# Group 5's q and k: cast on GpSimd and transposed by DMA instead of on TensorE

## The chip, the cores and the metric

The kernel runs on one core of one Trainium2 chip. The metric is the device time of one execution in microseconds, lower is better. The engines in this text: TensorE (PE, with its weight loads as PEld), VectorE (DVE), ScalarE (ACT), GpSimd (POOL) and SyncE (SP), which here does nothing but issue transfers.

## The reference

Chunked attention over 8 batches of 8 heads, 576 positions, head size 64, in chunks of 64, then a feed-forward layer with a squared ReLU:

```python
scores = scale * np.matmul(q_c, k_c.transpose(0, 1, 2, 4, 3))      # per chunk of 64
attn = np.exp(scores - max); attn = attn / (sum(attn) + 1e-09)
x = np.matmul(attn, v_c)  ->  (4608 tokens, 512)
h = np.maximum(x @ w_in, 0.0)                                       # 512 -> 2048
return (h * h) @ w_out                                              # 2048 -> 512
```

## The kernel before

The 4608 tokens are 18 groups of 256; two groups make a block of the feed-forward layer. While block j goes through the feed-forward layer, the attention of block j + 1 is slipped in between its matmuls, and the loads for block j + 2 are issued. A block has 48 slots, one after every four matmuls of TensorE; a plan says what is emitted in which slot. Scores need q and k with the head size on the partitions, so both must be transposed. Groups up to 5 do this on TensorE (`TA`), later ones by DMA (`C`, a cast to bf16 on GpSimd, then `TD`).

```python
FIRST_DMA_T = 6
...
in_pool = ctx.enter_context(tc.tile_pool(name="qk", bufs=5))
att_pool = ctx.enter_context(tc.tile_pool(name="att", bufs=3))
...
def cast_qk(g):                                     # C
    qkb = att_pool.tile([128, 2, 2 * H * D], BF16, name="qkb", bufs=2)
    state["qkb", g] = qkb
    for which in range(2):
        nc.gpsimd.tensor_copy(
            out=qkb[:, which], in_=qk[g][which].rearrange("p t h d -> p (t h d)"))

def transpose_qk_dma(g):                            # TD
    qkb = state.pop(("qkb", g))
    qkT = att_pool.tile([128, 2, 2, n_hp, 128], BF16, name="qkT", bufs=4)
    state["qkT", g] = qkT
    nc.sync.dma_start_transpose(
        out=qkT.rearrange("c w t h q -> c (w t h) q"),
        in_=qkb.rearrange("p w c -> p (w c)"))
...
elif j == 1:                                        # the plan of block 1
    loads = itertools.chain(*map(qk_pieces, far), v_pieces(far[0]))
    go_slots = range(14, 32)
    for slot, f in ((1, TA), (5, SC), (8, AV), (12, XT)):
        at(slot, f, grps[1])                        # group 3
    for i, g in enumerate(nxt):                     # groups 4, 5
        for slot, f in ((21 + 4 * i, TA), (28 + 2 * i, SC), (33 + 2 * i, AV),
                        (38 + 3 * i, XT)):
            at(slot, f, g)
    for i, g in enumerate(far):                     # groups 6, 7
        at(34 + 3 * i, C, g)
        at(36 + 3 * i, TD, g)
```

`SC` is the scores with their exponential, `AV` the values, `XT` the transpose of the attention's output for the feed-forward layer. Every load and every DMA transpose goes through SyncE's one queue, in program order.

The softmax here doesn't subtract the row's maximum and nothing guards it: scores larger than these inputs give would overflow.

Of the kernel before, what the change touches and what calls it, by code (L numbers as in the profile page):

```python
# [17 lines left out]
def kernel(  # L18
# [19 lines left out]
    GT = 256  # L38
    n_grp = n_tokens // GT
    blocks = [[g, g + 1] for g in range(0, n_grp, 2)]  # L40
    FIRST_DMA_T = 6
    FIRST_DMA_X = 6
    BT = GT * max(len(b) for b in blocks)

# [58 lines left out]
    def qk_pieces(g):  # L103
# [13 lines left out]
        qk[g] = (q_sb, k_sb)  # L117
        if g < FIRST_DMA_T:

# [15 lines left out]
    def v_pieces(g):  # L135

        for t, p, m, b, s in runs(g):
            yield lambda t=t, p=p, m=m, b=b, s=s: nc.sync.dma_start(  # L138
                out=v_even[g % NV][p:p + m, t, :, 0:D],
                in_=v[b, 0::2, s:s + m, :].rearrange("h s d -> s h d"))  # L140

        g0, g1 = GT * g, GT * (g + 1)
        first, last = (g0 + CT, g1) if g % 2 else (g0, g1 + CT)
        for n in range(2 * g, 2 * g + 3):
            lo, hi = max(first, 128 * n - 64), min(last, 128 * n + 64)
            if lo >= hi:
                continue
            p = lo - (128 * n - 64)
            for b, s, m in segments(lo, hi - lo):
                yield lambda n=n, p=p, m=m, b=b, s=s: nc.sync.dma_start(  # L150
                    out=v_odd[n % NO][p:p + m, :, 0:D],
                    in_=v[b, 1::2, s:s + m, :].rearrange("h s d -> s h d"))
                p += m

    def go(pieces):
        for f in pieces:
            f()
# [191 lines left out]
    C, TD = cast_qk, transpose_qk_dma  # L349
    SC, AV, XT = scores, values, transpose_x  # L350
# [24 lines left out]
    def ffn_in(j, parts):  # L375
        for c, n, ft in ((c, n, ft) for c, n, fts in parts for ft in fts):

            o, per = ft * n % 512, 512 // n
            if o == 0:
                h = ps_ffn.tile([128, 512], FP32, name="ps_ffn")  # L380
            mm_in(j, h, o, ft, c, n)
            if o + n == 512:
                relu2(j, h, ft + 1 - per, per, c)
            yield
# [7 lines left out]
    def ffn_out(j):  # L392
        gT = gTs.pop(j)
        n_tt = len(blocks[j]) * GT // 128
        for tt in range(n_tt):
            if j == len(blocks) - 1 and tt == n_tt - 1:

                for dma, c in ((nc.scalar, 0), (nc.sync, 256)):
                    o_ps = ps_ffn.tile([128, d_model], FP32, name="ps_ffn")
                    for ft in range(n_ft):  # L400
                        nc.tensor.matmul(  # L401
                            out=o_ps[:, 0:256],
                            lhsT=gT[:, ft, tt * 128:(tt + 1) * 128],
                            rhs=w_out_bf[:, ft, c:c + 256],
                            start=(ft == 0), stop=(ft == n_ft - 1))
                    o_sb = ffn_pool.tile([128, d_model], FP32, name="o_sb", bufs=4)
                    nc.vector.tensor_copy(out=o_sb[:, 0:256], in_=o_ps[:, 0:256])
                    store(dma, j, tt, o_sb[:, 0:256], slice(c, c + 256))
                continue
            o_ps = ps_ffn.tile([128, d_model], FP32, name="ps_ffn")  # L410
            for ft in range(n_ft):
                nc.tensor.matmul(  # L412
                    out=o_ps,
                    lhsT=gT[:, ft, tt * 128:(tt + 1) * 128],
                    rhs=w_out_bf[:, ft, :],
                    start=(ft == 0), stop=(ft == n_ft - 1))
                if ft == n_ft - 1:
                    o_sb = ffn_pool.tile([128, d_model], FP32, name="o_sb", bufs=4)
                    nc.scalar.copy(out=o_sb, in_=o_ps)  # L419
                    store(nc.gpsimd, j, tt, o_sb, slice(0, d_model))  # L420
                if ft % 4 == 3:
                    yield

    def ffn_out_by_ft(j):

        gT = gTs.pop(j)
        n_tt = len(blocks[j]) * GT // 128
        o_ps = [ps_ffn.tile([128, d_model], FP32, name="ps_ffn") for _ in range(n_tt)]

        def mm(tt, ft):  # L430
            nc.tensor.matmul(  # L431
                out=o_ps[tt],
                lhsT=gT[:, ft, tt * 128:(tt + 1) * 128],
                rhs=w_out_bf[:, ft, :],
                start=(ft == 0), stop=(ft == n_ft - 1))

        for ft in range(n_ft - 4):
            for tt in range(n_tt):
                mm(tt, ft)
            yield  # L440
        for tt in range(n_tt):
            for ft in range(n_ft - 4, n_ft):
                mm(tt, ft)
            o_sb = ffn_pool.tile([128, d_model], FP32, name="o_sb", bufs=4)
            nc.scalar.copy(out=o_sb, in_=o_ps[tt])
            store(nc.gpsimd, j, tt, o_sb, slice(0, d_model))
            yield

    def pieces(grps):
        for g in grps:  # L450
            yield from qk_pieces(g)
        for g in grps:
            yield from v_pieces(g)
# [44 lines left out]
    for j, grps in enumerate(blocks):  # L498
        nxt = blocks[j + 1] if j + 1 < len(blocks) else []
        far = blocks[j + 2] if j + 2 < len(blocks) else []  # L500
        plan = {}

        def at(slot, f, g):
            plan.setdefault(slot, []).append((f, g))

        if j == 0:
            loads, go_slots = pieces(far), range(17)
            for slot, f in ((22, TA), (25, SC), (26, AV), (28, XT)):
                at(slot, f, nxt[0])
            phases = [ffn_in(0, [(0, 512, range(2, n_ft))]), ffn_out_by_ft(0)]  # L510
        elif j == 1:
            loads = itertools.chain(*map(qk_pieces, far), v_pieces(far[0]))
            go_slots = range(14, 32)
            for slot, f in ((1, TA), (5, SC), (8, AV), (12, XT)):
                at(slot, f, grps[1])
            for i, g in enumerate(nxt):
                for slot, f in ((21 + 4 * i, TA), (28 + 2 * i, SC), (33 + 2 * i, AV),
                                (38 + 3 * i, XT)):
                    at(slot, f, g)
            for i, g in enumerate(far):  # L520
                at(34 + 3 * i, C, g)
                at(36 + 3 * i, TD, g)
            phases = [ffn_in(1, [(0, 256, range(n_ft)), (256, 256, range(n_ft))]), ffn_out(1)]
        else:
            loads, go_slots = pieces(far), range(32)
            slots = {SC: 9 if j == 3 else 8, AV: 11, XT: 15, C: 14, TD: 19}
            if j == 2:
                loads = itertools.chain(v_pieces(nxt[1]), loads)
                go_slots = [*range(14), 17, 18, *range(22, 32)]
                slots = {SC: 8, AV: 12, XT: 16, C: 16, TD: 21}  # L530
            for i, g in enumerate(nxt):
                at(slots[SC] + (3 * i if j == 2 else 0), SC, g)
                at(slots[AV] + 4 * i, AV, g)
                at(slots[XT] + 3 * i, XT, g)
            for i, g in enumerate(far):
                at(slots[C] + 2 * i, C, g)
                at(slots[TD] + 3 * i, TD, g)
            phases = [ffn_in(j, [(0, BT, range(n_ft))]), ffn_out(j)]
        slot = 0
        for phase in phases:  # L540
            for _ in phase:
                if slot in go_slots:
                    for f in loads:
                        f()
                        break
                for f, g in plan.get(slot, []):
                    f(g)
                slot += 1
        go(loads)
# [30 lines left out]
```

## Time and profile before

| | before |
|---|---|
| time, median of 3 runs | 294.34 us (294.0 to 294.53) |
| span of the profiled run | 292.4 us |
| TensorE busy | 98% |
| transposes of q, k on TensorE, one group | a piece of 1.01 us in the chain |
| GpSimd between its last store of block 0 and the cast of group 6 | idle for 20.6 us |

How to read it: TensorE has no gaps from 45 us on, so work taken from it shortens the span, unless the data that replaces the work comes later than TensorE wants it. A transfer "lands" when its data is all there: its issue plus the time from issue to landing. The slack of a transfer is the time from its landing to the moment when TensorE wants the data. One more pair of lines of the chain of waits in the kernel before (start in us, length, what) will serve as a ruler for all runs: the first matmuls of block 1 and of block 2.

```profile
49.03 0.97 PE ps_ffn L360 x8
...
84.71 7.77 PE ps_ffn L360 x36
```

Block 1, the only block in which the change moves work of TensorE, takes 84.71 - 49.03 = 35.68 us. Group 7's scores, on which the prediction turns, stand in block 2, so that block has to be measured as well: to the first matmuls of block 3, at 114.48 in the prediction's lines, it takes 29.77 us.

### The profile page before, as it was taken

Reading aid. Unit: us, or ns where it says so; the run is one execution under the profiler, and the core shown is the slowest. Engines: PE = TensorE matmul, PEld = TensorE weight load, DVE = VectorE, ACT = ScalarE, POOL = GpSimd, SP = SyncE. Lnnn points to the kernel's source line nnn. Section 1 sums busy time; section 2 is a strip of 40 time slices with the busy share of each in tenths; the row PEclk is TensorE's granted clock in tenths of the full one; section 3 lists DMA queues with packets and bytes.
Section 4 is the critical chain, followed back from the end, with each engine's and each line's share of the span. In section 5 each row is a group of like instructions: output and inputs, shape, how many; then the busy total and the mean of one; then the engine's idle time right before and its main releaser. Section 6 shows DMA issues by size and latency. Waiting matters only on the chain.

```text
span 292.4 us, 6471 instructions
## 1 busy us (share of the span) xinstructions
PE 285.6 (98%) x2661; PEld 141.7 (48%) x2661; DVE 111.0 (38%) x234; ACT 131.2 (45%) x214; POOL 66.8 (23%) x107
## 2 busy tenths in 40 slices
PE   7899999999999999999999999999999999999995
PEld 3454445885544444444444444444444444444444
DVE  0458413665414710571068105710472046104401
ACT  1557315775137513761376137612761276127410
POOL 2047824001510241042122113311043100230010
PEclk9999999999999999999999999999999999999999
DMA  7999999978999999999998899188999911331011
GB/s 233 248 349 366 352 294 255 345 160 192 214 165 209 211 213 206 250 198 232 263 232 170 189 231 214 37 184 211 201 209 224 202 39 36 74 72 36 0 74 72
DMA packets 145933, 56.00 MB, mean 191 GB/s; under 512 B 127024, under 2 KB 141616, under 8 KB 145904
## 3 DMA queue, kind: packets, MB, share of 16 engines
q1 hardware_dynamic: 142896, 46.28, 75.1%
q0 software_dynamic: 2864, 9.18, 10.2%
q8 instruction: 21, 0.34, 0.5%
q10 hardware_dynamic: 144, 0.13, 0.1%
q14 instruction: 8, 0.07, 0.1%
HBM read 36.70 MB, written 9.44 MB: 158 GB/s over the span
## 4 chain that ended last, share of the span: by engine, by line
PE 83%; DMA 8%; SPq 4%; POOL 2%; issue 0%; DVE 0%; DVEq 0%
PE ps_ffn L360 39%; PE ps_ffn L412 37%; DMA w_st<-in_moe_w_out_dram 4%; DMA w_st<-in_moe_w_in_dram 4%; PE ps_att L315 2%; SPq L138 2%; PE ps_att L291 2%; SPq L150 2%; PE ps_ffn L401 1%; PE ps_ffn L431 1%; PE ps_att L196 1%; POOL w_out_bf L179 1%; POOL w_in_bf L172 1%; PE ps_att L342 1%; POOL w_in_bf L168 1%
## 5 line engine op out<-in xcount | busy, mean ns | idle before, releaser
L360 PE MATMUL ps_ffn<-xT,w_in_bf 128*128 128x512 bf16 (+3 forms) x648 | 130.0, 356 | 0.2 <-POOL w_in_bf L168 0.2
L372 DVE TENSOR_TENSOR gT<-rl 128x512 bf16<-128x512 bf16 x144 | 71.2, 510 | 135.7 <-ACT rl L370 134.7
L412 PE MATMUL ps_ffn<-w_out_bf,gT 128*128 128x512 bf16 x496 | 109.3, 379 | 0.0
L370 ACT ACTIVATE rl<-ps_ffn 128x512 bf16<-128x512 f32 x144 | 85.1, 599 | 37.3 <-PE ps_ffn L360 35.8
L360 PEld LDWEIGHTS <-w_in_bf 128*128 128x128 bf16 x648 | 61.3, 98 | 60.4 <-POOL w_in_bf L168 0.9
L412 PEld LDWEIGHTS <-gT 128*128 128x128 bf16 x496 | 47.8, 98 | 56.3
L419 ACT COPY o_sb<-ps_ffn 128x512 f32<-128x512 f32 x31 | 18.2, 586 | 93.0 <-PE ps_ffn L412 93.0
L389 POOL DMA_DIRECT2D out_dram<-o_sb x39 | 21.2, 545 | 119.1 <-ACT o_sb L419 115.8
L270 POOL CAST qkb<-qk_sb 128x1024 bf16<-128x1024 f32 x24 | 25.8, 1085 | 76.2 <-DMA qk_sb<-in_q_dram 72.5
L323 DVE TENSOR_TENSOR x<-ps_att,rec 128x512 bf16<-128x512 f32 x36 | 24.9, 691 | 1.2
L298 ACT ACTIVATE e<-ps_att 128x1024 bf16<-128x1024 f32 x18 | 17.7, 1023 | 2.3 <-PE ps_att L291 2.3
L431 PE MATMUL ps_ffn<-w_out_bf,gT 128*128 128x512 bf16 x64 | 15.0, 379 | 0.3 <-POOL w_out_bf L179 0.3
L264 PE MATMUL ps_ffn<-zeros 128*128 128x512 bf16 x29 | 9.5, 466 | 1.3 <-POOL zeros L57 1.3
L179 POOL CAST w_out_bf<-w_st 128x1024 bf16<-128x1024 f32 x8 | 9.1, 1131 | 6.9 <-DMA w_st<-in_moe_w_out_dram 6.8
L315 PEld LDWEIGHTS <-e 64*64 64x64 bf16 x576 | 6.6, 107 | 7.5 <-DVE gT L372 2.1
L322 DVE RECIPROCAL rec<-ps_att 128x8 f32<-128x8 f32 x36 | 7.2, 199 | 7.1 <-PE ps_att L315 7.0
L431 PEld LDWEIGHTS <-gT 128*128 128x128 bf16 x64 | 6.0, 98 | 7.4 <-issue 0.6
L315 PE MATMUL ps_att<-ve_sb,e 64*64 64x65 bf16 x288 | 8.8, 196 | 0.1
L315 PE MATMUL ps_att<-vo_sb,e 64*64 64x65 bf16 x288 | 8.8, 196 | 0.0
L205 ACT COPY qkT<-ps_att 128x512 bf16<-128x512 bf16 x8 | 4.3, 589 | 9.7 <-PE ps_att L196 9.7
L172 POOL CAST w_in_bf<-w_st 128x1024 bf16<-128x1024 f32 x7 | 7.4, 1062 | 2.9 <-DMA w_st<-in_moe_w_in_dram 2.9
L291 PEld LDWEIGHTS <-qkT 64*64 64x64 bf16 x576 | 5.7, 108 | 4.7 <-issue 3.4
(33 smaller groups left out, 59.8 us busy)
## 6 DMA issues: line engine op xcount, KB each, us to landing
out_dram<-o_sb POOLq DMA_DIRECT2D x31, 256.0 KB, 4.0
qk_sb<-in_q_dram SPq DMA_DIRECT2D x20, 256.0 KB, 5.3
qk_sb<-in_k_dram SPq DMA_DIRECT2D x20, 256.0 KB, 5.4
ve_sb<-in_v_dram SPq DMA_DIRECT2D x32, 128.0 KB, 4.1
w_st<-in_moe_w_in_dram SPq DMA_DIRECT2D x8, 512.0 KB, 6.7
w_st<-in_moe_w_out_dram SPq DMA_DIRECT2D x8, 512.0 KB, 6.1
vo_sb<-in_v_dram SPq DMA_DIRECT2D x24, 128.0 KB, 3.6
qk_sb<-in_q_dram SPq DMA_DIRECT2D x4, 512.0 KB, 7.0
```

Source lines behind the costliest of these rows:

```text
L179: nc.gpsimd.tensor_copy(out=w_out_bf[:, 2 * i:2 * i + 2, :], in_=st)
L270: nc.gpsimd.tensor_copy(out=qkb[:, which], in_=qk[g][which].rearrange("p t h d -> p (t h d)"))
L298: nc.scalar.activation(out=e.rearrange("p a h t q -> p (a h t q)"), in_=ps, func=AF.Exp, scale=scale)
L315: nc.tensor.matmul(out=ps[64 * p:64 * p + 64, a, hp * (D + 1):(hp + 1) * (D + 1)], lhsT=e[64 * c:64 * c + 64, a, hp, t, :], rhs=vb[64 * c: ...
L323: nc.vector.tensor_tensor(out=x[:, t].rearrange("p h a d -> p a h d"), in0=o[:, :, :, 0:D], in1=rec.to_broadcast([128, 2, n_hp, D]), op=AL ...
L360: nc.tensor.matmul(out=h[:, o:o + n], lhsT=w_in_bf[:, dt, ft * 128:(ft + 1) * 128], rhs=xT[:, c // 128:(c + n) // 128, dt, :], start=(dt = ...
L370: nc.scalar.activation(out=rl, in_=h, func=AF.Relu)
L372: nc.vector.tensor_tensor(out=gTs[j][:, ft:ft + per, c:c + 512 // per], in0=r3, in1=r3, op=ALU.mult)
L389: eng.dma_start(out=out[b * S + s:b * S + s + m, cols], in_=o_sb[p:p + m, :])
L412: nc.tensor.matmul(out=o_ps, lhsT=gT[:, ft, tt * 128:(tt + 1) * 128], rhs=w_out_bf[:, ft, :], start=(ft == 0), stop=(ft == n_ft - 1))
L419: nc.scalar.copy(out=o_sb, in_=o_ps)
L431: nc.tensor.matmul(out=o_ps[tt], lhsT=gT[:, ft, tt * 128:(tt + 1) * 128], rhs=w_out_bf[:, ft, :], start=(ft == 0), stop=(ft == n_ft - 1))
```

## The change

Intent: relieve TensorE of one more group's transposes. Group 5 takes the way of the later groups. Its cast and its DMA transpose are emitted in slots 12 and 13, so they stand in the queues behind its values and ahead of the loads of groups 6 and 7; scores, values and x of groups 4 and 5 get other slots, to leave the transpose time to land. With the same constant the q and k of group 5 come in four loads with rows of 256 B instead of two with 512 B.

```diff
-    FIRST_DMA_T = 6
+    FIRST_DMA_T = 5
@@ block 1's plan
             for i, g in enumerate(nxt):
-                for slot, f in ((21 + 4 * i, TA), (28 + 2 * i, SC), (33 + 2 * i, AV),
-                                (38 + 3 * i, XT)):
+                for slot, f in ((28 + 6 * i, SC), (31 + 6 * i, AV), (36 + 5 * i, XT)):
                     at(slot, f, g)
+            for slot, f in ((12, C), (13, TD)):
+                at(slot, f, nxt[1])
+            at(21, TA, nxt[0])
             for i, g in enumerate(far):
                 at(34 + 3 * i, C, g)
-                at(36 + 3 * i, TD, g)
+                at(38 + 3 * i, TD, g)
```

## The prediction

> **What bounds the kernel now.** I read the page first, for the engine that is full, then the chain of work that ended last in order of time, then the SyncE queue in order of time, and last the view of one tile for the landing of single transfers.
>
> ```profile
> PE 285.6 (98%) x2661; PEld 141.7 (48%) x2661; DVE 111.0 (38%) x234; ACT 131.2 (45%) x214; POOL 66.8 (23%) x107
> DMA  7999999978999999999998899188999911331011
> ```
>
> TensorE is busy for 98% of the span, and the DMA row is full for the first 80% of it as well: two resources without slack on average, which is why a change that moves work from one to the other needs the dates of both. The chain (start, length, what; in us) shows that from 45 us on TensorE runs without a gap, so every microsecond taken from it, or added as a wait, is a microsecond of the end:
>
> ```profile
> 61.43 1.02 PE ps_att L196 x32
> 62.45 1.85 PE ps_ffn L360 x16
> 64.30 1.01 PE ps_att L196 x32
> ...
> 70.73 0.39 PE ps_att L315 x28
> 71.12 1.83 PE ps_ffn L412 x8
> ...
> 92.48 0.38 PE ps_att L291 x32
> 92.85 2.69 PE ps_ffn L360 x12
> 95.55 0.38 PE ps_att L291 x32
> ...
> 114.48 8.63 PE ps_ffn L360 x40
> ```
>
> Here 61.43 is the transpose of q, k of group 4, 64.30 that of group 5 (the piece that is removed), 70.73 the first values of group 4, 92.48 and 95.55 the scores of groups 6 and 7, and 114.48 the first matmuls of the fourth block (two groups make a block; a slot below is one step of four matmuls of a block's 48). The SyncE queue (start, time that issuing took, what) shows when each transfer could be given out:
>
> ```profile
> 49.25 3.13 SPq L123 DMA_DIRECT2D qk_sb<-in_q_dram  x1
> 52.43 2.07 SPq L123 DMA_DIRECT2D qk_sb<-in_k_dram  x1
> ...
> 62.86 1.16 SPq L150 DMA_DIRECT2D vo_sb<-in_v_dram  x2
> 64.06 0.60 SPq L131 DMA_DIRECT2D qk_sb<-in_q_dram  x1
> 64.71 0.58 SPq L131 DMA_DIRECT2D qk_sb<-in_k_dram  x1
> 65.33 2.76 SPq L131 DMA_DIRECT2D qk_sb<-in_q_dram  x1
> ...
> 78.74 7.62 SPq L277 DMA_TRANSPOSE qkT<-qkb  x2
> 86.40 1.22 SPq L138 DMA_DIRECT2D ve_sb<-in_v_dram  x2
> ```
>
> It has hardly a gap between 26 and 135 us: it issues the next transfer the moment the last is out. 49.25 and 52.43 are q, k of group 5, 64.06 is the first load of group 6, and 78.74 the two transposes by DMA of groups 6 and 7. The second of these two, from the tile's view (first line its issue, second its issue to landing):
>
> ```profile
> L277 SPq DMA_TRANSPOSE qkT<-qkb x1: 4457/4457/4457, 81.9 to 81.9; - x1
> DMA to landing us min/median/max: 10.3/10.3/10.3
> ```
>
> So group 7's q, k are ready at 81.90 + 10.27 = 92.17 and its scores begin at 95.55: a slack of 3.38 us. This is the number on which the prediction turns.
>
> **What the Trainium skill says.** "DMA: Bandwidth & Descriptors", section "Issuing engines are not separate DMA queues": transfers of all issuers run on the same 16 engines and interleave. The trace agrees: the two transposes landed 8.2 and 10.3 us after issue while three output stores of GpSimd were in flight, and 5.1 us after issue at 163.3 without one. The same page, "Specifications", gives 512 B as the least transfer for full rate. That bears on the loads of group 5, whose rows go from 512 B to 256 B; the trace agrees only roughly (next part). "Perfetto Trace Analysis", "DMA Instruction — HWDGE (DVE, Sync)": the profiled length of such an instruction is descriptor generation with the wait for the generator, not data movement. The trace agrees: the load at 65.33 took 2.76 us to issue, the one before it, of the same size, 0.58. So a long issue means [...]a transfer put in front delays all behind it. "TensorE: Matmul & The Clock Gate", section "Part 4: PE-mode transpose", gives some 275 ns for a whole 128x128 transpose in a kernel. That is a latency; here 32 of them, pipelined, take 1.01 us of the chain, and that is the figure I use.
>
> **The change part by part.**
> 1. Removed from TensorE: 32 transposes of group 5, 1.01 us of the chain. With them go two copies on VectorE (684 ns each) and two on ScalarE (589 ns each), both engines under half busy and not on the chain: worth nothing by themselves. Gain: 1.0 us, 0.35% of 294.3.
> 2. Moved on TensorE: scores of group 5 from slot 30 to 34, values of group 4 from 33 to 31, of group 5 from 35 to 37, transposes of x from 38 to 36 for group 4; the issues of the transposes by DMA of groups 6 and 7 go from 36 and 39 to 38 and 41, on SyncE in the same place behind group 6's values. The same work in another order. Scores to values of group 4 are 3 slots of small matmuls apart, some 1.4 us, against 1.02 us of exponential; the same distance stands without a gap for group 3 at 53 us. No cost.
> 3. Added to GpSimd: two casts of 1.04 us for group 5. GpSimd is idle for 20.6 us from its store at 49.95 to the cast at 71.1, so they lie free.
> 4. Loads of group 5 in four DMAs with 256 B rows instead of two with 512 B. SyncE time: the two took 3.13 + 2.07 = 5.2 us, four of 256 B rows in a full queue (90.33 to 95.00, and 116.22 to 121.06) take 4.7 to 4.8. Landing: those two landed 4.84 us apart from group 4's last (57.31 to 62.15) with stores beside them; four small ones later land in 4.7 to 5.0. Issue time is about even, and engines may need up to 1 us more. I take +0.6 us.
> 5. Added to the queue: one DMA transpose. Issues of this kind take 1.75 to 4.46 us, median 2.81. I take 2.8.
> The queue behind it, from group 6's loads on, is thus 0.6 + 2.8 = 3.4 us late.
>
> Two dates follow. Group 5's own: v of group 5 is issued by 64.0 + 0.6 = 64.6; its q, k have landed by about 63.3 and the second cast is done by 64.4, so the cast does not hold it up. Issue at 64.7, landing 5.1 to 7.2 us later (the rows at 163.3 and 165.1): 69.8 to 71.9, middle 70.8. The scores of group 5 now come at 70.73 + 0.39 + 0.91 - 1.01 - 0.38 = 70.6 (values of group 4 and one more slot come before, the transposes and the old place of the scores fall out). Wait about 0.2 us: the end stands at -0.8 us. Group 7's: 92.17 + 3.4 = 95.6, and its scores without waits would come at 95.55 - 1.01 = 94.5. The wait is 1.0 us, which is the whole gain: the end stands at 95.6 - 95.55, about 0. Waits of this sort don't add up. Each sets the least shift of the end, and the largest counts: 294.34 + 0.05, so **294.4 us**.
>
> **The rivals.**
> A. The transposition is hidden, full gain: 293.3 us. It needs a delay of the queue under 2.4 us. For it: the eight loads of groups 6 and 7 took 10.8 us to issue (64.06 to 74.83), against 9.6 to 9.8 for eight such loads at 116 and 142, so up to 1 us of clogging could vanish; and the busy row has holes around 68 and 74. Against it: the transpose alone blocks SyncE for at least 1.75 us and its half megabyte must run on the same engines.
> B. The wait is larger than the gain: if the transpose blocks the queue like the slow one (4.46 us) or group 5's loads cost the whole 1.1 us, the delay is 4.5 to 5.5 us and the end comes 1.1 to 2.1 us later, 295.4 to 296.4. Then further dates come close: the DMA transpose of x of group 7 lands at 109.72 for 114.48 (slack 4.8), that of q, k of group 9 at 118.99 for about 123.44 (slack 4.4). All of them have more slack than group 7's scores, so they only add if the delay grows on the way.
> C. The new wait is group 5's own, at the scores in slot 34. A landing at 72.5 would give an end at +0.9 us: 295.2. It is the likelier place of a wait if the casts or loads come late, and a wait there also moves group 7's scores back, so less is waited there.
> What speaks against any large effect: later than 150 us the queue has idle time of its own (7.6 us from 180.1 on), so a delay is made up, and TensorE work afterwards is unchanged.
>
> **Range and chances.** Best case -1.0 us (293.3), which is a hard floor, since only 1.01 us leave the chain; delays of the queue of 2.4 to 4.9 us, my eight in ten, give -1.0 to +1.5; with the spread of runs (294.0 to 294.5 before), 293.2 to 296.0. The floor makes faster by over 2% (5.9 us) all but impossible; slower by 2% needs a delay of the queue of 9 us or an unseen blocking between SyncE and GpSimd. Chances: 0.01, 0.965, 0.025.
>
> **What would show it.** Step 1: 96 transposes on that line instead of 128, in three pieces of 1.0 us in the chain. Step 5: a DMA transpose issued at about 64.7, issue 1.8 to 3.5 us, and the first load of group 6 at about 67.5 instead of 64.06. Dates: group 5's transposed q, k land at 69.8 to 71.9, those of group 7 at 95 to 96.5; between 94.5 and 95.6 TensorE's weight load of the scores waits for the DMA transpose. Wrong if: TensorE shows no wait in 65 to 100 us (rival A), the largest wait lies before 75 us (rival C), a first wait appears after 100 us, or GpSimd's casts of group 5 end after 65 us.

## The result, and the profile after

The changed kernel took 292.94 us (median of 4 runs, 292.81 to 293.16) beside 294.42 us (4 runs, 294.0 to 294.53). The ratio is 0.9953, with a 95% interval of 0.9936 to 0.997. (A ratio here is the mean time of one kernel's fast runs over that of the other's of the same rounds, so it is not quite the ratio of the medians quoted.) The gain is some 1.4 us; no gain had been forecast, and 292.94 lies just below the stated range of 293.2 to 296.0.

The page of the changed kernel, engines first:

```profile
PE 283.0 (97%) x2607; PEld 140.8 (48%) x2629; DVE 110.4 (38%) x232; ACT 130.3 (45%) x212; POOL 68.9 (24%) x109
```

GpSimd has two instructions more (the casts), TensorE the 32 transposes less. (The count of matmuls fell by 54, because some records are missing from this trace; the weight loads, which are all there, fell by 32.) Next the chain of waits after:

```profile
48.95 0.97 PE ps_ffn L360 x8
...
61.35 1.01 PE ps_att L196 x32
62.37 3.16 PE ps_ffn L360 x28
65.53 0.38 PE ps_att L291 x32
...
70.41 0.37 PE ps_att L291 x32
...
83.51 7.77 PE ps_ffn L360 x36
```

61.35 is the transposes of group 4; those of group 5 are gone, and the 28 matmuls at 62.37 run through where there had been 16 and 12. 65.53 and 70.41 are the scores of groups 4 and 5. Block 1 now takes 83.51 - 48.95 = 34.56 us, 1.12 less. Nothing is given back in block 2, which takes 29.77 us again (to 113.28). SyncE's queue after (start, time to issue, what):

```profile
62.93 1.15 SPq L150 DMA_DIRECT2D vo_sb<-in_v_dram  x2
64.25 2.98 SPq L277 DMA_TRANSPOSE qkT<-qkb  x1
67.30 0.56 SPq L131 DMA_DIRECT2D qk_sb<-in_q_dram  x1
...
80.31 5.44 SPq L277 DMA_TRANSPOSE qkT<-qkb  x2
```

The new transpose goes out at 64.25 and takes 2.98 us to issue; the first load of group 6 follows at 67.30, not at 64.06. So the queue was delayed about as predicted. But the two transposes of groups 6 and 7 now take 5.44 us to issue together, where they had taken 7.62. The tile's view of the transposed q, k has the landings, first for group 5:

```profile
L277 SPq DMA_TRANSPOSE qkT<-qkb x1: 2977/2977/2977, 64.3 to 64.3; - x1
DMA to landing us min/median/max: 5.1/5.1/5.1
```

and then for group 7:

```profile
L277 SPq DMA_TRANSPOSE qkT<-qkb x1: 2863/2863/2863, 82.9 to 82.9; - x1
DMA to landing us min/median/max: 6.6/6.6/6.6
```

Group 5 is ready at 64.25 + 5.13 = 69.38, 1.0 us before TensorE comes to its scores at 70.41. Group 7 is ready at 82.9 + 6.6 = 89.5, earlier than before (92.17) in spite of the delay, and almost 5 us before its scores at about 94.4. This is the riddle: a transfer that was put in front of a full queue made a later member of the queue come sooner.

### The profile page after: what moved, and what is told of

It reads as the page before. It is cut to its first block, busy times and chain, and to the rows that moved or that the text cites. A ratio compares the mean times of both kernels' runs of the same rounds, so it can differ in the third digit from the quotient of the medians.

```text
span 291.0 us, 6389 instructions
## 1 busy us (share of the span) xinstructions
PE 283.0 (97%) x2607; PEld 140.8 (48%) x2629; DVE 110.4 (38%) x232; ACT 130.3 (45%) x212; POOL 68.9 (24%) x109
## 4 chain that ended last, share of the span: by engine, by line
PE 81%; DMA 8%; SPq 4%; POOL 2%; DVE 1%; ACT 1%; issue 1%; DVEq 0%
PE ps_ffn L360 37%; PE ps_ffn L412 37%; DMA w_st<-in_moe_w_out_dram 4%; DMA w_st<-in_moe_w_in_dram 4%; PE ps_att L315 2%; SPq L138 2%; SPq L150 2%; PE ps_att L291 2%; PE ps_ffn L401 1%; PE ps_ffn L431 1%; POOL w_out_bf L179 1%; POOL w_in_bf L172 1%; PE ps_att L196 1%; PE ps_att L342 1%; ACT rl L370 1%
## 5 line engine op out<-in xcount | busy, mean ns | idle before, releaser
L360 PE MATMUL ps_ffn<-xT,w_in_bf 128*128 128x512 bf16 (+3 forms) x648 | 129.7, 356 | 0.1
L372 DVE TENSOR_TENSOR gT<-rl 128x512 bf16<-128x512 bf16 x144 | 72.0, 514 | 134.1 <-ACT rl L370 133.1
L412 PE MATMUL ps_ffn<-w_out_bf,gT 128*128 128x512 bf16 x480 | 108.2, 379 | 0.9 <-issue 0.2
L360 PEld LDWEIGHTS <-w_in_bf 128*128 128x128 bf16 x648 | 61.4, 98 | 60.2 <-POOL w_in_bf L168 0.7
L270 POOL CAST qkb<-qk_sb 128x1024 bf16<-128x1024 f32 x26 | 27.9, 1086 | 70.7 <-DMA qk_sb<-in_q_dram 66.5
L431 PE MATMUL ps_ffn<-w_out_bf,gT 128*128 128x512 bf16 x61 | 14.5, 379 | 0.7 <-issue 0.3
L205 ACT COPY qkT<-ps_att 128x512 bf16<-128x512 bf16 x6 | 3.2, 589 | 9.2 <-PE ps_att L196 9.2
```

What stands on the lines that cost most here:

```text
L270: nc.gpsimd.tensor_copy(out=qkb[:, which], in_=qk[g][which].rearrange("p t h d -> p (t h d)"))
L360: nc.tensor.matmul(out=h[:, o:o + n], lhsT=w_in_bf[:, dt, ft * 128:(ft + 1) * 128], rhs=xT[:, c // 128:(c + n) // 128, dt, :], start=(dt = ...
L372: nc.vector.tensor_tensor(out=gTs[j][:, ft:ft + per, c:c + 512 // per], in0=r3, in1=r3, op=ALU.mult)
L412: nc.tensor.matmul(out=o_ps, lhsT=gT[:, ft, tt * 128:(tt + 1) * 128], rhs=w_out_bf[:, ft, :], start=(ft == 0), stop=(ft == n_ft - 1))
L431: nc.tensor.matmul(out=o_ps[tt], lhsT=gT[:, ft, tt * 128:(tt + 1) * 128], rhs=w_out_bf[:, ft, :], start=(ft == 0), stop=(ft == n_ft - 1))
```

## The experiments

Two readings were on offer. HIDDEN: the DMA part costs the end nothing and the gain is TensorE's time. The prediction's: the delay of the queue reaches group 7's scores. LUCK and SCHEDULE, in the expectations, are two theories of group 7's landing: that its date differs from execution to execution, or that the order of the queue fixes it.

### before_again and before_third: the kernel before, new profiles

No edit. Expected of the first:

> The kernel before, unchanged, for a second profile. Theory LUCK (the date at which group 7's transposed q, k landed before, 92.17, was one draw of a spread of several us): it lands at another date by more than 1 us. Theory SCHEDULE (the order of the queue and of the stores fixes it): 92.2 within 0.5 us. Scores of group 7 at 95.5, span 292.4 within 0.3 in both.

Of the second:

> The kernel before, a third profile. LUCK: the landing of group 7's transposed q, k differs again from 92.17 and 85.74 by over 1 us, so its slack to the scores (3.4 and some 10.2 us in the first two profiles) is no property of the kernel. SCHEDULE: near one of the two.

Measured: 294.74 and 294.19 us (single runs). The tile's view for group 7's transpose, first of before_again:

```profile
L277 SPq DMA_TRANSPOSE qkT<-qkb x1: 2652/2652/2652, 79.4 to 79.4; - x1
DMA to landing us min/median/max: 6.3/6.3/6.3
```

then of before_third:

```profile
L277 SPq DMA_TRANSPOSE qkT<-qkb x1: 3293/3293/3293, 80.1 to 80.1; - x1
DMA to landing us min/median/max: 6.5/6.5/6.5
```

Landings at 85.7 and 86.6, where the first profile had 92.2, with TensorE's scores at 95.3 to 95.9 in all three. The slack of group 7 is 10.1 and 8.8 us here, not 3.4. The date in the first profile was one draw, and a late one. LUCK holds; SCHEDULE falls. What delayed that one execution is not shown: in it the two transposes took 7.6 us to issue, here 5.1 and 6.3 us from the first issue to the end of the second. Three or four output stores of GpSimd were in flight beside them in each of the three profiles, so their number alone does not explain it. The store issued at 82.2 was slow as well in the first profile, 8.9 us to landing, where the stores issued at 82.5 and 82.0 took 4.1 and 4.2 here. By the ruler, block 1 takes 35.79 us (before_again) and 35.68 (before_third).

### after_again and after_third: the changed kernel, new profiles

> The changed kernel, unchanged, for a narrow ratio and a second profile. Theory HIDDEN (the transposition by DMA costs the end nothing; the gain is the TensorE time alone): 1.1 us off, ratio 0.9962. If the 1.4 us of the first comparison are real, and something else than TensorE time gains too: ratio 0.9953 with an interval that leaves out 0.9962. Group 7 lands at 89.5 within 0.5 (SCHEDULE) or elsewhere by more than 1 us (LUCK).

> The changed kernel, a third profile. From the first matmul of block 1 to that of block 3: 64.04 us as in the first two, no wait. Landing of group 7's transposed q, k between 88 and 92, before its scores at about 94.4; that of group 5's at 69.0 to 70.2, before 70.4.

Measured: 293.33 us (6 runs, 293.04 to 293.5) beside 294.46 (11 runs, 294.07 to 295.83), ratio 0.9948, interval 0.9927 to 0.997; and a single run of 292.57. So the 1.4 us are confirmed in size, though the interval reaches to where HIDDEN put it (0.9962). Block 1 takes 34.55 and 34.57 us by the same two lines of the chain (49.34 to 83.89, and 48.71 to 83.28), block 2 29.78 and 29.77. (Blocks 1 and 2 together are 64.33 or 64.34 us by these lines in all three profiles of the changed kernel; the expectations' 64.04 was not taken from them.) Group 7 lands at 91.0 and 89.9, group 5 at 70.1 and 69.1. Over three profiles of each kernel, group 7's landing is at 88.2 in the mean before and 90.1 after; without the one late draw, 86.2 before. The delay of the queue was real, some 2 to 4 us. It ate into a slack that was 2.6 to 3 times as large in the two repeats as the first profile had shown.

### pe_only: TensorE's half

```diff
 # against the changed kernel
-    FIRST_DMA_T = 5
+    FIRST_DMA_T = 6
-            for slot, f in ((12, C), (13, TD)):
-                at(slot, f, nxt[1])
+            at(22, lambda g: state.update({('qkT', g): state['qkT', g - 1]}), nxt[1])
```

The result is wrong: group 5 computes with group 4's q and k.

> TensorE's part of the change alone: order of the slots as after, the 32 transposes of group 5 left out, but no cast, no DMA transpose and the old loads; group 5 takes group 4's q, k (wrong result on purpose). HIDDEN: as fast as the changed kernel within 0.2 us (293.0 to 293.4). If the DMA part costs something on the path after all: faster than the changed kernel by that cost. Scores of group 7 at 94.4 in both. It also measures what a visit of 32 transposes costs TensorE in all: 1.01 us by the piece of the chain, 1.1 if the change-over of the matmul stream is paid too.

Measured: 293.86 us (6 runs, 293.26 to 294.44), ratio 0.9966, interval 0.9944 to 0.9987. The ruler:

```profile
49.03 0.97 PE ps_ffn L360 x8
...
83.59 7.77 PE ps_ffn L360 x36
```

Block 1 takes 34.56 us. That is to 0.01 us the changed kernel's, so the DMA half takes nothing from block 1. Block 2 takes 29.78 us (to 113.37). From the first matmul of block 1 to the last weight load of the kernel it is 238.68 us, in three profiles of the changed kernel 238.53 to 238.69: the DMA half costs nothing later either. Group 7 landed at 83.4 in this profile. By the times it came out 0.5 us behind after_again, outside the 0.2 expected; 0.2 us of that is explained under three_loads. The rest may be the start, on which more below, but the runs without a profile don't show it.

### dma_only: the DMA half

```diff
 # against the kernel before
+    def spare_dma(g):                       # as transpose_qk_dma, into a tile nobody reads
+        ...
+            at(12, C, nxt[1])
+            at(13, spare_dma, nxt[1])
```

> The DMA part of the change alone: the kernel before with group 5's transposes kept on TensorE and, beside them, the two casts and the DMA transpose of group 5 into a spare tile that nobody reads, at the place in the queue where the change has it. HIDDEN: same as before within 0.2 us (ratio 1.000), first load of group 6 some 3 us later than before, yet group 7 lands before 95.5. Theory of the prediction (the delay of the queue is carried to group 7): group 7 lands at 95.0 to 96.5 and the end comes 0 to 1 us later, ratio 1.000 to 1.003.

Measured: 295.23 us (6 runs, 294.2 to 296.25), ratio 1.0014, interval 0.9987 to 1.004. First load of group 6 at 66.82 in a profile that was 1.6 us later already when block 1 began; group 7 lands at 84.5 + 7.2 = 91.7, its scores come at 97.1. The ruler, here with block 3 (the program is seven lines longer, so L360 is L367):

```profile
50.62 0.97 PE ps_ffn L367 x8
...
86.30 7.77 PE ps_ffn L367 x36
...
116.07 1.94 PE ps_ffn L367 x9
```

Block 1 takes 35.68 us, block 2, in which a wait of group 7's scores would stand, 29.77, both to the digit as before. To the last weight load it is 239.78 us, in three profiles of the kernel before 239.65 to 239.91. The times alone would not have settled this one: they allow -0.4 to +1.2 us. The ruler inside the trace does. (The four smaller loads are not in this run; they are in the changed kernel, which pe_only matches.) The start explains a part of the spread of the times: before block 1 begins, the kernel waits for its weights, and this date went from 48.7 to 51.1 us over the profiled runs (after_third and sc_early), though the program up to that point is the same.

So TensorE's half is worth 1.12 us and the DMA half 0, at the slack that these executions had. Left open were 0.2 to 0.3 us of the gain, and how much more the queue could have borne.

### three_loads: the last 0.2 us

By the traces, from the first matmul of block 1 to the last weight load of the kernel the change saves 1.20 us (means of three profiles each, 239.78 and 238.59; 1.12 of it in block 1, the rest is within what repeats differ by). From the start of that last weight load to the end of the span, the kernel before needs 3.84, 3.85 and 3.85 us, the changed one 3.63 in all three, though the work there is the same. At the very end SyncE waits for the semaphores of its transfers one after the other. Its waits, in the last microseconds of the kernel before:

```profile
SPq L575 <- DMA out_dram<-o_sb: 1.1, 1, 1.1
```

and of the changed kernel:

```profile
SPq L577 <- DMA out_dram<-o_sb: 0.9, 1, 0.9
```

The experiment adds to the kernel before three small loads on SyncE's queue, which is how many transfers the change adds there (two loads and the transpose):

```diff
+        if j == len(blocks) - 1:
+            for n in range(3):
+                at(2 + n, lambda n: nc.sync.dma_start(out=<spare 128x64>, in_=v[0, n, 0:128, :]), n)
```

> The kernel before with three small loads more on SyncE's queue, into tiles that nobody reads, early in the last block; TensorE's work is untouched. The trace so far shows SyncE at the very end waiting for its transfers' semaphores one after the other in a fixed order, and the changed kernel, which has three transfers more on that queue, is through 0.21 us sooner after the last weight load (3.63 against 3.84 us). If it is the place of the last store in that order: 3.63 us here too. If it comes from anything else in the change: 3.84.

Measured: 294.61 us (a single run, too coarse for this), 3.60 us from the last weight load to the end, and the same wait of SyncE is

```profile
SPq L580 <- DMA out_dram<-o_sb: 0.9, 1, 0.9
```

So the 0.2 us belong to the count of transfers. In the trace SyncE's transfers take eight semaphores in turn, and the waits at the end have the same order in the three traces, about 0.06 us from one to the next. In the changed kernel the last store's semaphore comes later in that order, so three more waits are over before it lands, and fewer follow. The same stretch fits in the halves: 3.84 us in pe_only, which has the transfers of the kernel before, and 3.80 in dma_only, which has one more. It is worth having noticed, but no merit of the transposition. Block 1 is at 35.68 us (49.50 to 85.18), and group 7 landed at 87.6, a fourth draw for the kernel before.

### td_x3: the suspected cost trebled

```diff
 # against the changed kernel
-            for slot, f in ((12, C), (13, TD)):
+            for slot, f in ((12, C), (13, TD), (13, lambda g: spare_dma(g, 2))):
```

> The suspected cost trebled: behind group 5's DMA transpose two more of the same kind into tiles that nobody reads. The first load of group 6 then goes out some 5.6 us later than in the changed kernel, at about 73. HIDDEN with a slack of 3.6 to 5 us (group 7 landed at 89.5 and 91.05 for scores at 94.4 and 94.7): group 7 lands at 95 to 96.6 and its scores wait 0.5 to 2 us, the end between 293.5 and 295.0. If the queue has far more room than that: 293.0 to 293.5 and no wait. If the prediction's sum were right for every transpose: 3 x 2.8 + 0.6 - 3.4 = 5.6 us later than before less nothing, near 298.

Measured: 296.49 us (4 runs, 293.67 to 298.71, one of them slow), ratio of the fast runs 1.0024, interval 0.9971 to 1.0077. The profiled run is fast. Its waits between 85 and 105 us:

```profile
PE ps_att L298 <- DMA qkT<-qkb: 1.8, 1, 1.8
```

Group 7 landed at 94.7, as expected, but the wait came one step earlier: group 6's transpose landed at 92.80, when TensorE had stood before the scores of group 6 since 91.0, and group 7 was then in time for its own at 95.9. Block 2 takes 2.15 us longer by the first matmuls of blocks 2 and 3 (31.92 us, where the changed kernel has 29.77); besides the 1.8 us, TensorE's weight loads waited 0.6 us for the DMA transpose of an x at the start of block 3. The wait has the expected size (0.5 to 2) at a neighbour of the group that I had named. So the mechanism of the prediction exists; in this profile it took two transposes more in the queue than the change puts there. It does not strike in every execution: the fastest of the four runs took 293.67 us.

### sc_early and sc_early_again: the old slots

```diff
 # against the changed kernel
-                for slot, f in ((28 + 6 * i, SC), (31 + 6 * i, AV), (36 + 5 * i, XT)):
+                for slot, f in ((28 + 2 * i, SC), (33 + 2 * i, AV), (38 + 3 * i, XT)):
```

> The change with one part undone: scores, values and x of groups 4 and 5 keep the slots that they had before (scores of group 5 in slot 30 instead of 34). TensorE comes to them at about 67.0 (68.09 less 1.12), while the DMA transpose lands at 69.4 to 70.1. If the date of this landing is what the moved slots pay for: a wait of 2.4 to 3.1 us at these scores, the end 1.3 to 2.0 us later than before, 2.4 to 3.1 later than the changed kernel (295.7 to 296.4). If the slots didn't matter: like the changed kernel, 293.0 to 293.5.

> The run with the old slots once more, for a profile in the fast state (the last one fell in a slow one, clock 0.989). The scores of group 5 at slot 30 wait for their DMA transpose: 2.4 to 3.1 us if it lands at 69.4 to 70.1, and the time from the first matmul of block 1 to that of block 3 grows by as much over the changed kernel's 64.04 us. If the wait also lowers the clock of TensorE, by more than the wait.

Measured: sc_early 297.58 us (4 runs, 295.69 to 301.26), ratio of the fast runs 1.0071, interval 1.003 to 1.0113; its profile fell in the slowest run. The repeat, 297.62 us, has a landing in the expected range (69.78). Its waits between 60 and 80 us:

```profile
PE ps_att L291 <- DMA qkT<-qkb: 2.9, 1, 2.9
```

and its stretches (length, busy us and instructions of each engine, granted TensorE clock, DMA share, GB/s):

```profile
68.00:70.00 2.00, 0.17 (x20) 0.17 (x24) 0.00 (x0) 0.00 (x0) 0.00 (x0) 1.00 1.02 230
70.00:72.00 2.00, 2.00 (x39) 1.14 (x29) 0.09 (x1) 1.53 (x2) 0.00 (x0) 0.54 1.11 242
72.00:74.00 2.00, 2.00 (x7) 0.58 (x5) 0.33 (x1) 0.00 (x0) 0.00 (x0) 0.60 1.19 233
74.00:76.00 2.00, 2.00 (x40) 1.05 (x40) 1.41 (x4) 0.00 (x0) 1.52 (x2) 1.00 1.14 218
```

The wait is 2.9 us, as forecast. But block 1 takes 88.17 - 48.95 = 39.22 us, 4.66 more than in the changed kernel. The column before the last two is the clock: after the idle stretch TensorE is granted 0.54 and 0.60 of its clock for 4 us, which loses 2 x 0.46 + 2 x 0.40 = 1.7 us; 2.9 + 1.7 = 4.6. The trace's own record of the clock has it at one half from 70.18 for 3.41 us. In sc_early's profile, a slow run with a wait of 3.6 us, it stood at one half for 6.83 us; in none of the other twelve profiles does it drop between 7 and 289 us. The Trainium skill, "TensorE: Matmul & The Clock Gate", section "Part 1: The HAM clock gate (the "warmup" mystery)", says that the clock halves after an idle window of about 3.4 us and comes back after some 3.4 us of work. The trace agrees on the 3.41 us of half clock and in kind on the rest; here 2.9 us of waiting were enough. None of the prediction's rivals had this in it: a wait of this length can be paid one and a half times. It is not always: two of the four runs of sc_early, 296.6 and 295.69 us, have mean clocks of 1.000 and 0.999, where by an estimate from this trace one such stretch (1.7 us of some 296) would leave 0.994.

So the moved slots are what makes the change pay. Without them the same transposition loses 0.7% (0.3 to 1.1).

### both_dma and both_dma2: group 4 as well

If one group's transposes are hidden, why not two? Group 4's go by DMA too, between the values of groups 4 and 5 in the queue.

```diff
 # against the changed kernel
-    FIRST_DMA_T = 5
+    FIRST_DMA_T = 4
-            loads, go_slots = pieces(far), range(17)                   # block 0
+            loads = itertools.chain(*map(qk_pieces, far), v_pieces(far[0]),
+                [lambda: C(far[0]), lambda: TD(far[0])], v_pieces(far[1]))
+            go_slots = range(13)
-                for slot, f in ((28 + 6 * i, SC), (31 + 6 * i, AV), (36 + 5 * i, XT)):
+                for slot, f in ((34 + 5 * i, SC), (37 + 5 * i, AV), (41 + 4 * i, XT)):
-            at(21, TA, nxt[0])
 # both_dma only: scores of group 7 in slot 13 instead of 11
```

> A version meant to beat both: q, k of group 4 by DMA as well, its transpose in the queue between the values of groups 4 and 5, scores of groups 4 and 5 in slots 34 and 39, values 37 and 42, x 41 and 45, scores of group 7 in slot 13 instead of 11. HIDDEN: another 1.12 us off TensorE, 291.9 to 292.4, ratio to before near 0.992. If the queue's delay is now over the slack (one more transpose, 2.9 us): a wait at the scores of group 5 or 7 of 0 to 2 us, and a time of 292.4 to 294.

> The version with both groups by DMA, with the scores of group 7 back in slot 11: in the last run they stood right behind the values of group 6 and waited some 0.6 us for VectorE to free a PSUM buffer. HIDDEN: TensorE ahead of the kernel before by 2 x 1.12 us from the third block to the end, 292.0 to 292.6, ratio about 0.992. If group 7's landing (92.1 in the last run) comes after some 94: a wait there and less gain.

Measured: both_dma 293.62 us (6 runs, 292.65 to 295.08), ratio 0.9967, interval 0.9938 to 0.9997. Block 1 takes 33.44 us (49.66 to 83.10), 2.24 less than before, exactly two visits. Then 0.6 us are lost in block 2. The chain there (after the last piece come the scores of group 7):

```profile
96.05 0.69 DVE x L323
...
96.89 0.45 PE ps_att L291 x32
```

The scores of group 7 follow VectorE's work on the values of group 6: I had moved them right behind those values, and they waited for a PSUM buffer. That was my own slip. both_dma2 undoes it: 295.17 us (6 runs, 292.97 to 297.5), reported ratio 1.0039, interval 0.9999 to 1.0079. Its profile, the fastest of the six, keeps the full lead through block 2 and loses half of it at the start of block 3:

```profile
PE ps_ffn L360 <- DMA xT<-x: 1.0, 1, 1.0
```

The DMA transpose of group 7's x landed at 112.85, after TensorE wanted it at 111.8; that is the next date in the row that the prediction had listed (109.72 for 114.48). Two of its six runs have clocks of 0.992 and 0.994 and times above 297, like the runs with a long wait above; their traces were not taken, so that this is the same effect is a guess. Neither version is faster than the changed kernel beyond the spread, and both vary more. The changed kernel stays the best of those tried; whether other slots would let the second group pay is not shown.

## Why the prediction was wrong

- What leaves TensorE: the mechanism was right, its size a tenth short. The piece of the chain is 1.01 us, but block 1 shrank by 1.12 us (from the 35.68 of all profiles with the old transposes but before_again, which has 35.79) in all profiles of the changed kernel and in pe_only. The missing 0.11 us show in the chain: 16 and 12 matmuls took 1.85 + 1.42 = 3.27 us on either side of the transposes, 28 without the interruption take 3.16.
- Copies, moved slots, casts: as predicted. VectorE and ScalarE are off the path, the casts ran at 60.6 in GpSimd's idle time, and the moves cost nothing: 1.01 + 0.11 us account for all of the 1.12. (No run makes the moves alone.)
- Loads with 256 B rows: group 5's last landed 4.5, 4.1 and 5.0 us after group 4's in three profiles, against 4.8, 3.4 and 4.1 before. I had added 0.6 us; the means differ by 0.4, which is within what repeats differ by. (My "4.7 to 5.0" for later small loads was misread: by the same measure the first three later groups took 5.0, 6.0 and 4.8.)
- Issue of the DMA transpose: 2.98, 3.59 and 2.90 us in three profiles, predicted 2.8. First load of group 6 at 67.3, predicted 67.5. Right. I had also compared with a transpose at 163.3 "without" an output store beside it: the trace has one there, issued at 163.78 and landed at 168.15. So that stores slow the transposes is not shown.
- Group 5's own date: predicted 69.8 to 71.9 for scores at 70.6, measured 69.1 to 70.1 for 70.1 to 70.7. No wait instead of 0.2 us.
- Group 7's date is the step that failed: "92.17 + 3.4 = 95.6 ... The wait is 1.0 us, which is the whole gain". The delay was sound, the date it was added to was not: the slack of 3.4 us in the sum was 10.1 and 8.8 in the two repeats. 92.17 came from one execution; three more gave 85.7, 86.6 and 87.6 (the last with three loads more, much later). With those, 3.4 us of delay land group 7 at 89 to 91, which is where it landed (89.5, 91.0, 89.9), in front of 94.5. The wait at group 7's scores was 0. Rival A was the true one, for another reason than the two that I had given it: the delay was not under 2.4 us, the slack was larger.
- "A hard floor, since only 1.01 us leave the chain": wrong twice. 1.12 us left, and the end itself became 0.2 us shorter by the count of transfers. 1.20 + 0.21 = 1.41 us by the traces, and 0.47% of 294.4 is 1.38.
- Rival B's sum does not follow: a slow transpose or slow loads alone, by its own numbers, make a delay of 5.1 or 3.9 us, both together 5.6; it says 4.5 to 5.5.
- Not foreseen: that a long wait can also halve the clock. Whether it would at the waits that rivals B and C had in mind (1 to 2 us) is not shown; in td_x3's profile 1.8 us left the clock whole.

## What to carry to other kernels

A date read from one profile can be a draw, as here: before a forecast turns on a slack of a few microseconds, take the same date from several executions, transfers above all. To judge a change smaller than the spread of the times, find a ruler inside the trace, such as the distance between two matmuls on either side of the change; here it repeated to 0.1 us while the times ran over 1.8. And when work goes from the full engine to a queue, move its consumers back in the same step, since a wait of 3 us on TensorE cost 4.7 us in one profile here.

## What the Trainium skill lacked or had wrong

- "TensorE: Matmul & The Clock Gate", "Part 4: PE-mode transpose", gives the time of one transpose, some 275 ns in a kernel. What a batch of 32 takes from a stream of matmuls is not there: 1.12 us, 0.11 of it for the change-over.
- The same page, "Part 1": the clock halves after an idle window of about 3.4 us. A wait of 2.9 us was enough in one profile here, and cost 1.7 us more; two other runs of the same kernel kept mean clocks of 0.999 and 1.000.
- "DMA: Bandwidth & Descriptors", "DMA Transpose (X-bar)", has no time for a transpose inside SBUF beside other traffic; the page only gives rates under "Latency and other measured facts", 261 GB/s with a middle dimension that is not contiguous and some 350 to 400 otherwise, estimates of 2.0 and 1.3 to 1.5 us for this half megabyte. Here it took 1.55 to 5.44 us to issue and 4.0 to 10.3 us to land.
- "DMA: Bandwidth & Descriptors", "Specifications": at least 512 B for the full rate. What smaller rows cost in a queue that other things hold up is not there: with 256 B group 5's loads landed 4.1 to 5.0 us after group 4's, with 512 B 3.4 to 4.8.
- No page says how far the landing of one transfer varies between executions of one kernel: 85.7 to 92.2 us for the same transpose.
- No page has what the order of a program's own semaphore waits at its end is worth: the place of the last transfer's semaphore made 0.2 us (3.84 and 3.60 us for the same work).
